# POOL's queue issues the later heads, global values and global queries, and the last seven weight splits stand one per slot

## Chip, cores and metric

One core of one Trainium2 chip runs the whole kernel. The metric is the time of one execution on the device in microseconds, and the number compared is the median of several runs.

## What is computed

The input is attention with a window and a few global tokens, followed by a two-layer feed-forward block. There are 8 batches of 8 heads with 512 local and 32 global tokens and head dimension 64.

```
s_g   = scale * q_g @ concat(k_g, k_l).T
out_g = softmax(s_g) @ concat(v_g, v_l)
s_ll  = where(|i - j| <= 32, scale * q_l @ k_l.T, -1e9)
a_l   = softmax(concat(scale * q_l @ k_g.T, s_ll))
out_l = a_l @ concat(v_g, v_l)
x = concat(out_g, out_l), heads side by side   # 4352 rows of 512
h = max(x @ w_in, 0)                           # w_in 512 x 2048
out = (h * h) @ w_out                          # w_out 2048 x 512
```

Queries, keys and values are float32. The weights are float64; the chip gets each as two 32-bit words and rebuilds a float32 from them.

## The kernel before

**Slots.** The work runs in slots t = 0, 1, 2 ... A slot holds one "head" t, which is half of one head of one batch (256 queries), 128 of them in all, and one eighth m = t - 9 of a block of 256 rows of the feed-forward part (17 blocks, the first of them in slots 9 to 16). Within a slot PE transposes the probabilities of head t-1 (tile `pt`), computes the scores of head t (`s`), two halves of the first matrix product (`h`), the product of probabilities and values of head t-1 (`xa`), the scores of the global queries (`gs`) and the second matrix product of eighth m-1 (`o`). ACT and DVE make what PE needs next: the softmax (`prob`, `st`), copies of `pt` into `ph` and `pl`, the activated rows `r`, `gh`, `gl`, and so on.

**Two halves of each number.** Heads up to 15 and the first block are computed in plain float32. From head 16 and from block 1 on, each operand is split into a rounded half and the rest: for a head, `split_head` makes `hi` and `lo` from `raw` with one ACT copy and three DVE subtractions; for a weight, `w_split` makes the pair `ws` from `wf` with one ACT copy and one DVE subtraction. There are 32 weight chunks. The table PLAN says at which of four places of a slot a chunk is rebuilt ("b") or split ("s"); `w_need` makes up what a product needs before the table has come to it.

**Loads.** `load_head(t)` brings head t into `raw`. Heads from 16 on use a pool of two buffers with the tag "raw", and it is called two slots ahead. The last rebuilt weight, `wf31`, takes one of these two buffers (`w_abs`), and holds it until it is split. `g_load(t)` brings the global queries of the next four heads (`qr`, one buffer) in slots t = 3, 7, 11 ..., and from t = 15 on copies them with ACT and DVE into `qgz`; this stands directly behind `split_head(t+1)`. `g_load_v` brings the global values (`gv`, one buffer). SP's queue issues all of these, the weights and the stores of the results.

**Order.** From slot 17 on (FREE), PE, DVE and ACT take their instructions in the order in which the program writes them, through the class InOrder; before that, and on SP's and POOL's queues throughout, a scheduler orders them. Recorded instructions all have line 52, the helper's.

Of the kernel before, what the change touches and what calls it, by code (L numbers as in the profile page):

```python
# [16 lines left out]
P = 128  # L17
# [9 lines left out]
LAG = 9  # L27
NPLAIN = 16

PLAN = [",,,b", "b,,,b", "b,,,b", "b,,b,", "b,,b,", "b,,b,", "b,,b,", "b,b,,b", "b,b,,b", "bb,bb,bb,bb", "bb,bb,bb,bb", "bbs,bb,bbs,bbs", "bbs,bbs,bbs,bbs", "bbs,bbs,bbs,bbs", "bbs,bbs,bs,s", "ss,s,s,s", "ss,s,s,s", "s,,s,", "s,,s,", "s,,s,", "s,,s,", "s,,s,", "s,,s,"]  # L30
FREE = (17, 17, 17)
LOOK = 2
SQ = (2, 3, 4, 5, 14, 15)
# [4 lines left out]
def f(ap):  # L38
    return ap.bitcast(F32)
# [19 lines left out]
def attention_moe(  # L59
# [8 lines left out]
):  # L68
    nc = tc.nc
    pe, ve, ac = InOrder(tc, nc.tensor), InOrder(tc, nc.vector), InOrder(tc, nc.scalar)  # L70
    PSUM = bass.MemoryType.PSUM
    cp = ctx.enter_context(tc.tile_pool(name="cp", bufs=1))
    wp = ctx.enter_context(tc.tile_pool(name="wp", bufs=WCH))
    p2 = ctx.enter_context(tc.tile_pool(name="p2", bufs=2))
    p1 = ctx.enter_context(tc.tile_pool(name="p1", bufs=1))
    ps_h = ctx.enter_context(tc.tile_pool(name="ps_h", bufs=2, space=PSUM))
    ps_o = ctx.enter_context(tc.tile_pool(name="ps_o", bufs=1, space=PSUM))
    ps_a = ctx.enter_context(tc.tile_pool(name="ps_a", bufs=1, space=PSUM))

    heads = {}  # L80

    def plain(t):
        return t < NPLAIN
# [3 lines left out]
    def w_take(n):  # L87
        w_bufs["free"] -= n

    def load_head(t):  # L90
        if plain(t):
            w_take(1)
            raw = wp.tile([P, 1024], F32, tag="w", name=f"raw{t}")[:, :PK]
        else:
            raw = p2.tile([P, PK], F32, tag="raw", name=f"raw{t}")
        if t == 0:
            nc.sync.dma_start(raw[:, : QC + KC], pk[t, :, : QC + KC])
        else:
            nc.sync.dma_start(raw, pk[t])
        heads[t] = dict(raw=raw)  # L100

    load_head(0)
    con = cp.tile([P, P + 4 * WIN], F32, name="con")

    half = P + 2 * WIN
    nc.sync.dma_start(con[:, P:half], consts[:, P:half])
    load_head(1)
    nc.sync.dma_start(con[:, :P], consts[:, :P])
    nc.sync.dma_start(heads[0]["raw"][:, QC + KC :], pk[0, :, QC + KC :])
    load_head(2)  # L110
    load_head(3)
    ident, masks = con[:, :P], con[:, P:]
# [4 lines left out]
    sg = cp.tile([P, 2, 640], F32, name="sg")  # L117
    qgz = cp.tile([P, 512], F32R, name="qgz")
    prob = [cp.tile([P, 2 * WIN], F32, name=f"prob{i}") for i in range(2)]
    pt = ps_a.tile([P, 512], F32, name="pt")  # L120
    nc.gpsimd.memset(f(qgz), 0.0)
    nc.gpsimd.memset(sg[:, :, 608:], 0.0)
    nc.vector.memset(pt[96:, 256:], 0.0)

    def split_head(t):
# [139 lines left out]
    def g_load(t):  # L265

        b, grp = t // 16, (t // 4) % 2

        def cols(z, j):
            return bass.AP(z.tensor, z.offset + 64 * j, [list(z.ap[0]), [256, 2], [160, 2], [1, 32]])  # L270

        src = qg[b, grp].rearrange("p (a b) n -> p a b n", a=2)
        if plain(t):
            qz = p1.tile([P, 512], F32, tag=("ph", "gvl", "gvh", "ph")[t // 4], name=f"qz{t}")
            nc.gpsimd.memset(qz, 0.0)
            qr = p1.tile([P, 2, 2, 32], F32, tag="qr", name=f"qr{t}")
            (nc.sync if t else nc.scalar).dma_start(qr, src)
            nc.gpsimd.tensor_copy(cols(qz, 0), qr)
        else:
            qz = qgz  # L280
            qr = p1.tile([P, 2, 2, 32], F32, tag="qr", name=f"qr{t}")
            nc.sync.dma_start(qr, src)
            ac.copy(cols(qgz, 0), qr)
            ve.tensor_sub(cols(qgz, 1), qr, f(cols(qgz, 0)))
        state["qz"] = qz
# [26 lines left out]
    def g_load_v(t, pair):  # L312
        gv = p1.tile([P, 640], F32, tag="gv", name=f"gv{t}_{pair}").rearrange("p (c n) -> p c n", c=5)
        src = vg[t // 16, 2 * ((t // 4) % 2) + pair]
        nc.sync.dma_start(gv, src.rearrange("(c p) n -> p c n", p=P))
        state["gv"] = gv

    def g_split_v(t, pair):
# [238 lines left out]
    def w_tick(t, place):  # L557
        if t < len(PLAN):
            for c in PLAN[t].split(",")[place]:
                {"b": w_pass, "s": w_chunk}[c]()  # L560
# [14 lines left out]
    def w_done(m):  # L575
        w_used.update(range(4 * m, 4 * m + 4))
        for i in (4 * m, 4 * m + 2):
            w_free(i)

    g_load(0)  # L580
    for t in range(4, 8):
        load_head(t)
# [6 lines left out]
    for t in range(NSTEP + LAG + 1):  # L589
# [55 lines left out]
        if live:  # L645
            if t % 2 == 1:
                g_evac(t)
            if t % 4 == 3 and t + 1 < NT:
                g_load(t + 1)
        elif t == NT:  # L650
            state["gs"] = None
        if live and t % 4 == 3 and (t // 8) % 2 == 1:
            d = t if t % 8 == 3 else t + 2
            for at, *job in (
                (d, 2, g_load_v, 0),
                (d + 1, 3, g_soft),
                (d + 1, 1, g_exp),
                (d + 2, 3, g_norm),
                (d + 2, 1, g_tr),
                (d + 3, 5, g_tr_last),  # L660
                (d + 3, 4, g_rest),
                (d + 3, 3, g_split_v, 0),
                (d + 3, 2, g_load_v, 1),
                (d + 3, 1, g_av, 0),
                (max(d + 4, 17), 3, g_x, 0),
                (d + 5, 2, g_split_v, 1),
                (max(d + 6, 17), 1, g_av, 1),
                (max(d + 7, 18), 3, g_x, 1),
            ):
                place, job, *args = job  # L670
                jobs.setdefault((at, place), []).append((job, t, *args))
# [21 lines left out]
        if 8 * NGR - 2 <= m < 8 * NGR:  # L693
            cols = (slice(0, 224), slice(224, HALF))[m % 2]
# [76 lines left out]
```

## Time and profile before

| | |
|---|---|
| median of 3 runs | 1068.83 us (1068.21 to 1069.07) |
| the profiled execution's own time | 1068.82 us |
| its span, first to last instruction | 1067.0 us |
| PE busy | 1050.4 us |
| DVE busy | 856.3 us |
| ACT busy | 753.1 us |
| POOL busy | 3.9 us in 14 instructions |

The profile gives, for one execution, when each instruction of each engine ran, and for an engine's idle time what ended it. An issue of a transfer is an instruction of a queue (SPq); its landing is told apart from it. Slots can be read from PE's row of instructions: each begins with the four transposes into `pt`.

### The profile page before, as it was taken

To read this page: it belongs to the slowest core of one execution; us is meant where nothing else is said; L and a number is where in the kernel's file an instruction comes from. 1 tells how busy PE (TensorE), PEld (TensorE's weight loads), DVE (VectorE), ACT (ScalarE), POOL (GpSimd) and SP (SyncE) were. 2 spreads that over 40 slices of the span, in tenths; PEclk is the share of its full clock that TensorE was granted. 3 is DMA by queue.
4 is the path that set the end of the run, shared out by engine and by line. 5 is a ranking of instruction groups with operands and counts; after the bars stand their busy time and mean duration, and the time that the engine had idled before them with its cause. 6 is when DMAs were issued, how large, how long until landed. Compare 5 with 4: busy or idle time off the path is not lost.

```text
span 1067.0 us, 21142 instructions
## 1 busy us (share of the span) xinstructions
PE 1050.4 (98%) x7568; PEld 941.7 (88%) x7568; DVE 856.3 (80%) x2687; ACT 753.1 (71%) x1901; POOL 3.9 (0%) x14
## 2 busy tenths in 40 slices
PE   7999999999999999999999999999999999999998
PEld 6776889999998989998999989999999989999896
DVE  5698988898888989988888888888888888874321
ACT  5898877778777776778777777777777787774322
POOL 1000000000000000000000000000000000000000
PEclk9999999999999999999999999999999999999999
DMA  9772132223222322222322222223221322201000
GB/s 372 310 263 74 57 106 76 71 80 98 68 89 64 103 65 83 74 91 77 94 71 82 86 72 76 90 66 100 78 89 55 94 86 66 88 29 33 13 20 20
DMA packets 54312, 96.78 MB, mean 91 GB/s; under 512 B 4288, under 2 KB 29376, under 8 KB 54208
## 3 DMA queue, kind: packets, MB, share of 16 engines
q1 hardware_dynamic: 54064, 95.37, 27.2%
q8 instruction: 60, 0.98, 0.4%
q14 instruction: 44, 0.36, 0.1%
q10 hardware_dynamic: 144, 0.07, 0.0%
HBM read 86.51 MB, written 8.91 MB: 89 GB/s over the span
## 4 chain that ended last, share of the span: by engine, by line
PE 87%; ACT 7%; DVE 4%; issue 1%; DMA 0%; ACTq 0%
PE o L52 33%; PE h L52 32%; PE xa L52 7%; PE s L52 6%; PE pt L52 5%; PE gxo L52 2%; PE gs L52 2%; ACT prob L52 1%; DVE prob L52 1%; ACT r L52 1%; ACT ph L52 1%; ACT hi L52 1%; ACT ot L52 1%; PE gt L52 1%; ACT sg L52 0%
## 5 line engine op out<-in xcount | busy, mean ns | idle before, releaser
L52 PE MATMUL h<-x_h,ws 128*128 128x256 f32 x2048 | 388.9, 283 | 0.0
L52 PEld LDWEIGHTS h<-x_h,ws 128*128 128x128 f32 x2048 | 327.0, 191 | 0.5
L52 PE MATMUL o<-ws,gh 128*128 128x512 f32 x1024 | 321.3, 395 | 0.0
L52 PE MATMUL h<-x_l,ws 128*128 128x256 f32 x1024 | 289.1, 282 | 0.1
L52 PEld LDWEIGHTS o<-ws,gh 128*128 128x128 f32 x1024 | 185.5, 188 | 34.6
L52 PE MATMUL o<-ws,gl 128*128 128x512 f32 x512 | 202.6, 396 | 0.0
L52 PEld LDWEIGHTS h<-x_l,ws 128*128 128x128 f32 x1024 | 195.9, 191 | 0.9 <-DVE x_l L52 0.4
L52 ACT CAST ph<-pt 128x256 fp32r<-128x256 f32 x448 | 141.1, 341 | 67.7 <-PE pt L52 60.8
L52 ACT ACTIVATE prob<-prob,st 128x224 f32<-128x224 f32 x270 | 127.8, 475 | 61.2 <-DVE st L52 59.1
L52 ACT ACTIVATE r<-h 128x512 f32<-128x512 f32 x136 | 81.4, 599 | 112.3 <-PE h L52 112.3
L52 PEld LDWEIGHTS o<-ws,gl 128*128 128x128 f32 x512 | 96.2, 188 | 22.7
L52 DVE CUSTOM_DVE_ANT_0 prob<-s,con 128x224 f32<-128x224 f32 x256 | 90.0, 386 | 24.5 <-PE s L52 23.2
L52 DVE TENSOR_TENSOR gl<-r,gh 128x512 fp32r<-128x512 f32 x128 | 87.9, 686 | 23.3 <-ACT gh L52 20.5
L52 ACT CAST hi<-raw 128x864 fp32r<-128x864 f32 x112 | 102.5, 915 | 1.4
L52 DVE TENSOR_TENSOR r<-h,r 128x512 f32<-128x512 f32 x82 | 56.7, 692 | 51.9 <-ACT r L52 50.6
L52 PE MATMUL xa<-ph,hi 128*64 128x128 f32 x448 | 87.3, 238 | 1.6 <-DVE ph L52 1.2
L52 DVE TENSOR_TENSOR hi<-raw,hi 64x352 fp32r<-64x352 f32 x224 | 82.5, 368 | 6.4
L52 ACT CAST gh<-r 128x512 fp32r<-128x512 f32 x128 | 79.1, 618 | 9.1 <-DVE r L52 8.7
L52 DVE TENSOR_TENSOR ph<-pt,ph 64x128 fp32r<-64x128 f32 x224 | 79.6, 355 | 7.0
L52 DVE TENSOR_TENSOR lo<-raw,hi 128x448 fp32r<-128x448 f32 x112 | 69.6, 622 | 15.3 <-ACT hi L52 12.5
L52 PE MATMUL pt<-con,prob 128*128 128x128 f32 (+1 forms) x512 | 78.2, 274 | 0.7 <-ACT prob L52 0.5
L52 DVE TENSOR_SCALAR prob<-prob,st 128x224 f32<-128x224 f32 x242 | 70.7, 334 | 4.1
(80 smaller groups left out, 1572.7 us busy)
## 6 DMA issues: line engine op xcount, KB each, us to landing
raw<-in_pk_dram SPq DMA_DIRECT2D x127, 432.0 KB, 3.2
wr<-in_w_dram SPq DMA_DIRECT2D x32, 512.0 KB, 7.9
gv<-in_vg_dram SPq DMA_DIRECT2D x32, 320.0 KB, 3.3
out_dram<-ot SPq DMA_DIRECT2D x32, 256.0 KB, 2.2
qr<-in_qg_dram SPq DMA_DIRECT2D x31, 64.0 KB, 2.8
out_dram<-ot SPq DMA_DIRECT2D x8, 64.0 KB, 1.7
con<-in_consts_dram SPq DMA_DIRECT2D x2, 224.0 KB, 5.1
raw<-in_pk_dram SPq DMA_DIRECT2D x1, 304.0 KB, 3.2
```

Of the source, the lines that this page charges most:

```text
L52: r = method(*args, **kwargs)
```

## The change

Three things are edited. POOL's instructions go through InOrder as well, so that its queue runs in the order in which the program is written. The loads of heads from 16 on, of all global values and of the global queries from slot 15 on are issued by POOL's queue instead of SP's. In PLAN, the weight splits from slot 17 on stand differently: before, two in each of slots 17, 18 and 19 and one in slot 20 were left to make; now one stands in each of slots 17, 19, 20, 21 and 22 and two in slot 23.

```diff
-... "ss,s,s,s", "s,,s,", "s,,s,", "s,,s,", "s,,s,", "s,,s,", "s,,s,"]
+... "ss,s,s,s", "s,,,", ",,,", "s,,,", "s,,,", "s,,,", "s,,,", "s,,s,"]
...
+    po = InOrder(tc, nc.gpsimd)
...
-            nc.sync.dma_start(raw, pk[t])
+            (nc.sync if plain(t) else po).dma_start(raw, pk[t])
...
-    nc.gpsimd.memset(f(qgz), 0.0)
-    nc.gpsimd.memset(sg[:, :, 608:], 0.0)
+    po.memset(f(qgz), 0.0)
+    po.memset(sg[:, :, 608:], 0.0)
...
         if plain(t):
...
-            nc.gpsimd.memset(qz, 0.0)
+            po.memset(qz, 0.0)
...
-            nc.gpsimd.tensor_copy(cols(qz, 0), qr)
+            po.tensor_copy(cols(qz, 0), qr)
         else:
...
-            nc.sync.dma_start(qr, src)
+            po.dma_start(qr, src)
             ac.copy(cols(qgz, 0), qr)
             ve.tensor_sub(cols(qgz, 1), qr, f(cols(qgz, 0)))
...
     def g_load_v(t, pair):
...
-        nc.sync.dma_start(gv, src.rearrange("(c p) n -> p c n", p=P))
+        po.dma_start(gv, src.rearrange("(c p) n -> p c n", p=P))
```

What follows are rows of the two programs as they are queued, with the semaphores that a row waits for; a number after a tile's name is the head or slot that it belongs to, the one after the underscore only counts tiles. DMAHW and DMASW are semaphores of landings.

The first place is the queue that loads. On SP's queue before, the global queries of heads 20 to 23 (`qr20`) stood among the weights:

```order
L406 DMA wr18_546<-in_w_dram 128x1024 [waits DMAHW6_49,PE_49]
L406 DMA wr19_568<-in_w_dram 128x1024 [waits DMAHW7_49,PE_49]
L282 DMA qr20_1358<-in_qg_dram 128x128 [waits DMAHW2_49,DMAHW0_49,DVE_49]
L406 DMA wr20_598<-in_w_dram 128x1024 [waits DMAHW1_49]
L406 DMA wr21_616<-in_w_dram 128x1024 [waits PE_49]
```

That is long before head 20 itself, which follows here, with the queries `qr24` ahead of head 22:

```order
L99 DMA raw20_1155<-in_pk_dram 128x864 [waits DMAHW0_49,DMAHW3_49,DVE_49,Activation_49]
L99 DMA raw21_1271<-in_pk_dram 128x864 [waits DMAHW3_49,DMAHW4_49,DVE_49,Activation_49]
L282 DMA qr24_1790<-in_qg_dram 128x128 [waits DVE_49]
L315 DMA gv15_1_1479<-in_vg_dram 128x5x128 [waits DMAHW7_49,DVE_49,Activation_49]
L99 DMA raw22_1388<-in_pk_dram 128x864 [waits DVE_49,PE_49]
L99 DMA raw23_1513<-in_pk_dram 128x864 [waits DMAHW4_49,DVE_49,Activation_49]
L99 DMA raw24_1612<-in_pk_dram 128x864 [waits DMAHW1_49,DMAHW7_49,DVE_49,Activation_49]
```

On POOL's queue now, at the same place of the program:

```order
L52 DMA raw20_1152<-in_pk_dram 128x864 [waits DMASW6_49,DVE_49,Activation_49]
L52 DMA raw21_1262<-in_pk_dram 128x864 [waits DMASW0_49,DVE_49,Activation_49]
L52 DMA qr20_1349<-in_qg_dram 128x128 [waits DMASW4_49]
L52 DMA raw22_1376<-in_pk_dram 128x864 [waits DMASW1_49,DVE_49,Activation_49]
L52 DMA gv15_1_1467<-in_vg_dram 128x5x128 [waits DMASW7_49]
L52 DMA raw23_1501<-in_pk_dram 128x864 [waits DMASW3_49,DVE_49,Activation_49]
L52 DMA raw24_1603<-in_pk_dram 128x864 [waits DMASW5_49,DVE_49,Activation_49]
L52 DMA raw25_1705<-in_pk_dram 128x864 [waits DMASW6_49,DVE_49,Activation_49]
L52 DMA qr24_1787<-in_qg_dram 128x128 [waits DMASW2_49]
L52 DMA raw26_1826<-in_pk_dram 128x864 [waits DVE_49,PE_49]
```

The queries `qr20` moved behind head 21 and `qr24` behind head 25. Each head from 18 to 25 now waits for the last reads (DVE, ACT) of the head directly in front of it, since they share one buffer; before, that ended with head 21, and head 22 took the buffer of `wf31`, which now goes to head 26 (the row that waits for DVE and PE).

The second place is ACT's queue in slot 19, from the evacuation of `xa18` to the copy of `pt` for head 19. Before:

```order
L52 CAST x_h_88<-xa18_1330 64x256 [waits PE_49]
L52 CAST hi20_1350<-raw20_1155 128x864 [waits DMAHW3_49]
L52 COPY sg_91<-gs18_1232 64x288 [waits PE_49]
L52 CAST qgz_92<-qr20_1358 128x2x2x32
L52 CAST gh10_1374<-r10_1345 128x512 [waits Activation_49]
L52 CAST ws30_1378<-wf30_835 128x512 [waits DVE_49]
L52 CAST pth15_1386<-gt15_1381 128x512 [waits PE_49]
L52 CAST ph19_1413<-pt_95 128x256 [waits PE_49]
```

Now:

```order
L52 CAST x_h_88<-xa18_1321 64x256 [waits PE_49]
L52 CAST hi20_1341<-raw20_1152 128x864 [waits DMASW0_49]
L52 COPY sg_91<-gs18_1226 64x288 [waits PE_49]
L52 CAST qgz_92<-qr20_1349 128x2x2x32 [waits DMASW2_49]
L52 CAST gh10_1365<-r10_1336 128x512 [waits Activation_49]
L52 CAST pth15_1374<-gt15_1369 128x512 [waits PE_49]
L52 CAST ph19_1401<-pt_95 128x256 [waits DVE_49,PE_49]
```

The split `ws30` left this place, and the copy into `qgz` got a wait for the landing of `qr20`.

The third place is ACT's queue in slot 23, from the same evacuation on. Before:

```order
L52 CAST hi24_1782<-raw24_1612 128x864 [waits DMAHW1_49]
L52 COPY sg_91<-gs22_1673 64x288 [waits PE_49]
L52 CAST qgz_92<-qr24_1790 128x2x2x32 [waits DMAHW5_49]
L52 CAST gh14_1806<-r14_1777 128x512 [waits DVE_49]
L52 ACTIVATE gxs15_1_1824<-gxo15_1_1810,gst15_1198 64x128 [waits PE_49]
L52 CAST ph23_1850<-pt_95 128x256 [waits PE_49,Activation_49]
```

Now:

```order
L52 CAST hi24_1779<-raw24_1603 128x864 [waits DMASW6_49]
L52 COPY sg_91<-gs22_1667 64x288 [waits PE_49]
L52 CAST qgz_92<-qr24_1787 128x2x2x32 [waits DMASW0_49]
L52 CAST gh14_1803<-r14_1774 128x512 [waits DVE_49]
L52 CAST ws31_1807<-wf31_864 128x512 [waits Activation_49]
L52 ACTIVATE gxs15_1_1824<-gxo15_1_1810,gst15_1195 64x128 [waits PE_49]
L52 CAST ph23_1850<-pt_95 128x256 [waits PE_49]
```

The order is the same but for the split `ws31`, which came in from slot 20.

More of the change, by code (lines that the diff above doesn't have):

```diff
@@ L28 @@
 NPLAIN = 16
-PLAN = [",,,b", "b,,,b", "b,,,b", "b,,b,", "b,,b,", "b,,b,", "b,,b,", "b,b,,b", "b,b,,b", "bb,bb,bb,bb", "bb,bb,bb,bb", "bbs,bb,bbs,bbs", "bbs,bbs,bbs,bbs", "bbs,bbs,bbs,bbs", "bbs,bbs,bs,s", "ss,s,s,s", "ss,s,s,s", "s,,s,", "s,,s,", "s,,s,", "s,,s,", "s,,s,", "s,,s,"]
+PLAN = [",,,b", "b,,,b", "b,,,b", "b,,b,", "b,,b,", "b,,b,", "b,,b,", "b,b,,b", "b,b,,b", "bb,bb,bb,bb", "bb,bb,bb,bb", "bbs,bb,bbs,bbs", "bbs,bbs,bbs,bbs", "bbs,bbs,bbs,bbs", "bbs,bbs,bs,s", "ss,s,s,s", "ss,s,s,s", "s,,,", ",,,", "s,,,", "s,,,", "s,,,", "s,,,", "s,,s,"]
 FREE = (17, 17, 17)
```

## Prediction

> **What bounds the kernel now.** I read the page's span and busy times first.
>
> ```profile
> span 1067.0 us, 21142 instructions
> PE 1050.4 (98%) x7568; PEld 941.7 (88%) x7568; DVE 856.3 (80%) x2687; ACT 753.1 (71%) x1901; POOL 3.9 (0%) x14
> ```
>
> PE idles for 16.6 us in all, so nothing that only feeds it faster can gain more. Next I cut the run into slots, at PE's four transposes, and asked for each engine's busy time in stretches: slots 16, 19 and 20, then slots 35 and 36, which hold the same jobs as 19 and 20 but no weight splits. The columns are the stretch in us, its length, and the busy time of PE, PEld, DVE, ACT and POOL.
>
> ```profile
> 97.51:106.97 9.46, 9.01 (x41) 6.31 (x40) 7.52 (x20) 7.64 (x18) 0.00 (x0) 1.00 0.27 81
> ...
> 122.95:131.57 8.62, 7.96 (x60) 7.15 (x59) 8.11 (x26) 7.80 (x20) 0.00 (x0) 1.00 0.18 53
> 131.57:141.36 9.79, 9.08 (x71) 7.66 (x69) 8.74 (x26) 7.73 (x19) 0.00 (x0) 1.00 0.35 105
> ...
> 156.09:164.13 8.04, 8.04 (x68) 7.45 (x67) 7.61 (x24) 5.24 (x14) 0.00 (x0) 1.00 0.33 98
> ...
> 246.93:255.05 8.12, 7.96 (x60) 7.14 (x59) 6.60 (x25) 6.46 (x17) 0.00 (x0) 1.00 0.17 54
> 255.05:263.65 8.60, 8.55 (x70) 7.55 (x69) 7.35 (x23) 6.59 (x16) 0.00 (x0) 1.00 0.32 98
> ```
>
> Slots 19 and 20 take 8.62 + 9.79 = 18.41 us, their counterparts 8.12 + 8.60 = 16.72 us. In slot 19 DVE is busy for 8.11 us, about as long as a slot without splits lasts: there, for a moment, DVE and ACT set the pace. The excess, 1.69 us, is what weight splits cost after slot 16.
>
> Then the loads: the page's issues with the median from issue to landing, what SP's queue waited for, the landings of `qr` (minimum, median, maximum), and POOL's two kinds of instruction, which have nothing to do with loads but are all that POOL does now.
>
> ```profile
> raw<-in_pk_dram SPq DMA_DIRECT2D x127, 432.0 KB, 3.2
> ...
> qr<-in_qg_dram SPq DMA_DIRECT2D x31, 64.0 KB, 2.8
> ```
>
> ```profile
> SPq L99 <- DVE hi L52: 626.7, 109, 21.1
> ...
> DMA to landing us min/median/max: 2.5/2.8/9.2
> ...
> 0.73 0.52 POOL L121 MEMSET qgz<- 128x512 f32 x1 [0.29 <-POOLq L761]
> ...
> 3.81 0.29 POOL L278 COPY qz<-qr 128x128 f32<-128x128 f32 x1 [1.08 <-DMA qr<-in_qg_dram]
> ```
>
> SP's queue stood still in 109 head loads until DVE had read the old head; a load there holds whatever is queued behind it, and I take POOL's queue to do the same.
>
> **The change part by part.** *The splits.* Three of them leave slots 17 to 19, one stays in slot 20, and slots 21, 22 and 23 get one, one and two. Out come up to 1.69 us; since slot 20 keeps its one, I take 1.3. Slot 23 (156.09 above) has DVE busy for 7.61 of 8.04 us, and two splits of about 0.6 us each (rows below) don't fit into that; but one falls behind the wait below and is counted there, so I put 0.3 us on slots 21 to 23.
>
> *The wait for `qr20`.* Before, these queries were on the chip long ahead. Now their load stands behind that of `raw21`, which waits until DVE has read `raw20`. ACT copies `qr20` into `qgz` before that moment:
>
> ```profile
> 130.85 0.30 ACT L52 CAST qgz<-qr 128x128 fp32r<-128x128 f32 x1
> 131.57 0.61 ACT L52 CAST ws<-wf 128x512 fp32r<-128x512 f32 x1
> ...
> 131.08 0.75 DVE L52 TENSOR_TENSOR hi<-raw,hi 64x352 fp32r<-64x352 f32 x2
> 133.15 0.69 DVE L52 TENSOR_TENSOR ws<-wf,ws 128x512 fp32r<-128x512 f32 x1
> ```
>
> DVE's last read ends at 131.08 + 0.75 = 131.83 and ACT wants the queries at 130.85, 0.98 us earlier. Call P the time from that read to their landing. Then ACT stands still for P + 0.98 us, with `gh`, `pth` and `ph` queued behind it, and DVE with its own part of `qgz`, then `gl`, `pth`, `pl` and `ph`.
>
> P is two issues and a landing, and no row shows POOL issue one. From below: the shortest landing, 2.5, and two issues of 0.3 (POOL's copy) make 3.1. From above: the landing of the head ahead of it, 3.2, and then a whole landing of 2.5, as if the two ran one after the other, make 5.7; the 9.2 belongs to the first slots, when all weights are loaded too. Less than nothing is excluded, since the order forces a landing after the read. I choose 4.2: two issues of 0.5, as POOL's 0.52 memset, and the 3.2 of the head's load, with which the queries share the engines. The Trainium skill, "DMA: Bandwidth & Descriptors", section on latency and other measured facts, gives about 1 us to the first byte for a transfer issued by GpSimd against about 0.6 by SP: by that P is 4.6 and, with both waits, the sum 0.8 us longer; no run here shows it yet.
>
> What that costs PE is read from slots 35 and 36, where no split is in the way:
>
> ```profile
> 254.12 0.30 ACT L52 CAST qgz<-qr 128x128 fp32r<-128x128 f32 x1
> ...
> 255.73 1.30 ACT L52 CAST ph<-pt 128x256 fp32r<-128x256 f32 x4
> 257.05 0.26 ACT L52 CAST pth<-gs 64x128 fp32r<-64x128 f32 x1
> ...
> 254.35 0.75 DVE L52 TENSOR_TENSOR hi<-raw,hi 64x352 fp32r<-64x352 f32 x2
> ...
> 257.34 0.29 DVE L52 TENSOR_TENSOR pth<-gs,pth 64x128 fp32r<-64x128 f32 x1 [0.24 <-ACT pth L52]
> ...
> 258.92 0.74 DVE L52 TENSOR_TENSOR ph<-pt,ph 64x128 fp32r<-64x128 f32 x2
> ...
> 259.81 0.31 PE L52 MATMUL xa<-ph,hi 128*64 128x256 f32 x1
> ```
>
> From the copy to the end of DVE's last piece of `ph`, at 259.66, there are 5.54 us, and PE uses it 0.15 us later: PE has no lead here. Some 0.55 us of the 5.54 are short idle times ahead of ACT's and DVE's `pth` that a late start takes up (0.24 of them in the row above, the rest ahead of ACT's). So PE is late by P + 0.98 - 0.55, rounded P + 0.4 = **4.6 us**.
>
> *The wait for `qr24`.* The same in slot 23, since `raw25` waits for `raw24`: both are in one buffer as long as `wf31`, now split in slot 23, holds the other.
>
> ```profile
> 162.26 0.30 ACT L52 CAST qgz<-qr 128x128 fp32r<-128x128 f32 x1
> 162.46 0.62 ACT L52 CAST gh<-r 128x512 fp32r<-128x512 f32 x1
> 164.34 0.36 ACT L52 ACTIVATE gxs<-gxo,gst 64x128 f32<-64x128 f32 x1 [1.26 <-PE gxo L52]
> 164.85 1.29 ACT L52 CAST ph<-pt 128x256 fp32r<-128x256 f32 x4 [0.15 <-PE pt L52]
> ...
> 162.51 0.77 DVE L52 TENSOR_TENSOR hi<-raw,hi 64x352 fp32r<-64x352 f32 x2
> ...
> 164.00 0.68 DVE L52 TENSOR_TENSOR gl<-r,gh 128x512 fp32r<-128x512 f32 x1
> ...
> 166.63 0.74 DVE L52 TENSOR_TENSOR ph<-pt,ph 64x128 fp32r<-64x128 f32 x2
> ...
> 168.40 0.28 PE L52 MATMUL xa<-ph,hi 128*64 128x256 f32 x1
> ```
>
> DVE's read ends at 163.28; with P = 4.2 the copy starts at 167.48 instead of 162.26, 5.2 us late. Behind it come `gh` to 168.3, the split `ws31` with its 0.5 us of ACT to 168.8, `gxs` and then `ph` from 169.2 to 170.5; DVE, with `gl` and 0.6 us of `ws31`, ends its last piece of `ph` at about 171.7. PE wanted it at 168.40: **3.35 us** late, or P - 0.85. Here PE has a lead of some 2 us, since ACT and DVE idle for 1.26 and more after the copy.
>
> *Later groups.* From head 26 on there are two buffers again, and the queries' load waits for a head one slot older:
>
> ```profile
> 185.42 0.77 DVE L52 TENSOR_TENSOR hi<-raw,hi 64x352 fp32r<-64x352 f32 x2
> ...
> 192.20 0.30 ACT L52 CAST qgz<-qr 128x128 fp32r<-128x128 f32 x1
> ```
>
> That read ends at 186.19, 6.0 us ahead of the copy: more than P, so nothing is paid. If the cover went, the price would be P - 6.0, less PE's lead of 2, in each of 25 groups. *The heads with one buffer*, 22 to 25, have to land in less time than before:
>
> ```profile
> 148.51 0.77 DVE L52 TENSOR_TENSOR hi<-raw,hi 64x352 fp32r<-64x352 f32 x2
> ...
> 153.84 0.92 ACT L52 CAST hi<-raw 128x864 fp32r<-128x864 f32 x1
> ```
>
> From 149.28 to 153.84 there are 4.56 us for a landing of 3.2 and an issue of 0.5. That holds, with 0.9 to spare. *Global values* are loaded three slots ahead of use and cost nothing; the same for the stores, alone on SP's queue with the weights now.
>
> *Before slot 17* the scheduler put ACT's and DVE's instructions in another order, as the weights no longer share a queue with heads. PE's order there is the same but for one swap. In slot 16 PE idles for 9.46 - 9.01 = 0.45 us; I take 0, and 1.5 us to either side, about three such gaps.
>
> The sum: -1.3 + 0.3 + 4.6 + 3.35 = 6.95, rounded 7.0 us on the profiled execution's own 1068.82 (span 1067.0 and 1.8 around it). That equals the median of 1068.83, so the forecast is **1075.8 us**. With P = 3.1 the waits are 3.5 and 2.25, the sum 4.75 and the time 1073.6; with P = 5.7 they are 6.1 and 4.85, the sum 9.95 and the time 1078.8.
>
> **The rivals.** *A: faster, because ACT gets to the copy later than I think.* If the scheduler's new order before slot 17 and the three splits less let PE run ahead of ACT and DVE, the copy is reached after the landing and both waits are hidden. This decides once ACT's copy comes P = 4.2 us behind DVE's read; today it comes 0.98 us ahead of it, and the very next row of DVE waits for the same copy. Then only the 1.3 us and slot 16's 0.45 remain: 1067.1 us. Against it: copy and read hang on the same `hi` copy of ACT, so they move together.
>
> *B: POOL's queue is slow, and the wait comes back in every group.* If issuing waits for gaps in DVE's work, P grows by a DVE row of up to 0.7 us per issue, to 5.6, which is in the range above. At P = 7 the sum is 12.75 and the time 1081.6; beyond P = 8 all 25 later groups pay, and with P = 9 they add 25 x 1.0 us to 16.55 us, for 1110 us. The Trainium skill, "SBUF — State Buffer", section "Who interferes with whom", states such a rule: a transfer issued by GpSimd is starved while DVE runs in a mode that takes both pairs of ports, and one issued by SP is not. Against it here: in the two places DVE itself comes to stand still behind the copy, and the rows ahead are subtractions of two operands.
>
> *C: only one wait shows.* If PE's lead in slot 24 is 4 us rather than 2, the second wait is hidden, and with P near 3.1 the sum is -1.3 + 0.3 + 3.5 = 2.5: 1071.3 us; less still, if the early slots gain.
>
> **How the numbers follow.** A measurement of this kernel can tell 0.2%, some 2.1 us, from no change. My forecast's mechanism has a chance of 0.70, A 0.08, B 0.13 (half of it within 1081.6), C 0.09. A is faster in 0.07 of its 0.08 and otherwise the same; of C, 0.06 is the same and 0.03 slower; forecast and B are slower. So faster 0.07, same 0.07, slower 0.86. The range goes from 1071.3, where C begins, to 1081.6, the middle of B; the forecast's own is 1072.1 (1073.6 less the early 1.5) to 1080.3.
>
> **What would show it.** In the changed profile ACT's copy into `qgz` in slots 19 and 23 would have an idle time of 4 to 6 us ahead of it, ended by the landing of `qr`; PE would idle for some 3 to 5 us ahead of `xa` in slots 20 and 24; slots 17 to 19 would be without PE's 0.66 us; from slot 26 on every slot would have its old length. I am wrong if these waits aren't there, if the idle time ahead of `qgz` is there but PE runs on, or if ACT waits for `qr` or `raw` in later groups too.

## The result, and the profile after

The changed kernel takes 1079.63 us (median of five runs, 1079.39 to 1080.52) against 1068.83 us (1068.21 to 1069.38) before: 10.8 us more, a ratio of 1.0102 with a 95% interval of 1.0088 to 1.0116. The profiled execution took 1080.52 us, 11.7 more than that of before.

Both waits are there. The page of the changed kernel, its span and busy times:

```profile
span 1078.8 us, 21127 instructions
...
PE 1055.1 (98%) x7568; PEld 945.4 (88%) x7568; DVE 857.2 (79%) x2687; ACT 752.3 (70%) x1901; POOL 106.9 (10%) x186
```

PE is busy 4.7 us longer than before, with as many products; 7 of the 11.7 us are idle time, and the rest is the same work done more slowly. Where ACT and DVE waited for the queries (time in all, how often, the longest):

```profile
ACT qgz L52 <- DMA qr<-in_qg_dram: 11.3, 2, 6.0
...
DVE qgz L52 <- ACT qgz L52: 8.1, 2, 4.1
```

Twice, and not once in a later group. The rows of DVE, POOL, ACT and PE around both places, from the timeline of the changed kernel (start, duration, operation, and in brackets the idle time ahead):

```profile
130.34 0.75 DVE L52 TENSOR_TENSOR hi<-raw,hi 64x352 fp32r<-64x352 f32 x2
...
131.64 0.54 POOL L52 DMA_DIRECT2D raw<-in_pk_dram  x1 [6.74 <-DVE sg L52]
132.17 0.54 POOL L52 DMA_DIRECT2D qr<-in_qg_dram  x1
...
135.38 0.30 ACT L52 CAST qgz<-qr 128x128 fp32r<-128x128 f32 x1 [5.29 <-DMA qr<-in_qg_dram]
...
137.68 0.25 PE L52 MATMUL xa<-ph,hi 128*64 128x128 f32 x1 [2.40 <-DVE ptl L52]
...
139.91 0.37 PE L52 MATMUL xa<-pl,hi 128*64 128x128 f32 x1 [1.93 <-DVE pl L52]
...
169.49 0.77 DVE L52 TENSOR_TENSOR hi<-raw,hi 64x352 fp32r<-64x352 f32 x2
...
174.35 0.30 ACT L52 CAST qgz<-qr 128x128 fp32r<-128x128 f32 x1 [5.98 <-DMA qr<-in_qg_dram]
...
176.38 0.37 PE L52 MATMUL xa<-ph,hi 128*64 128x128 f32 x1 [2.62 <-ACT ph L52]
...
177.76 0.37 PE L52 MATMUL xa<-pl,hi 128*64 128x128 f32 x1 [0.91 <-DVE pl L52]
```

DVE's last read of `raw20` ends at 131.09, and ACT has the queries at 135.38: the time called P is 4.3 us here, and 4.1 us (170.26 to 174.35) at the second place, against the 4.2 that the prediction chose. The sum is the forecast one, its parts are not: POOL starts the head's issue 0.55 us after the read, which no term held, and takes 0.54 us over it, and 3.2 us after the start of their own issue the queries have landed. The profile counts a landing from the start of its issue, so the prediction's second issue of 0.5 us was already in its 3.2; that the lag of 0.55 us stands in its place is luck.

Slots 19, 20 and 23 to 25 by the stretches view (the columns are those of the prediction; the three numbers behind POOL's are the granted clock, the share of the time in which the transfer engines were busy, and GB/s):

```profile
122.95:131.05 8.10, 7.95 (x60) 7.14 (x58) 7.19 (x26) 6.14 (x16) 0.55 (x1) 1.00 0.21 57
131.05:146.56 15.51, 11.18 (x71) 9.48 (x69) 9.27 (x26) 7.91 (x19) 1.33 (x3) 0.78 0.10 33
...
161.19:169.81 8.62, 8.39 (x68) 7.44 (x67) 7.75 (x23) 4.87 (x13) 0.54 (x1) 1.00 0.16 53
169.81:183.49 13.68, 10.14 (x57) 8.65 (x56) 8.99 (x28) 6.38 (x16) 1.60 (x3) 0.75 0.23 69
183.49:190.78 7.29, 7.29 (x56) 6.69 (x55) 5.62 (x19) 4.97 (x14) 0.54 (x1) 1.00 0.20 63
```

Slot 20 grew from 9.79 to 15.51 us and slot 24 from 7.30 to 13.68; every slot from 26 on has its old length to within some hundredths. But slot 20 idles for 4.3 us only, and PE's 71 matmuls, which kept it busy for 9.08 us before, now take 11.18. The clock column says why. Cut finer:

```profile
135.50:138.22 2.72, 0.30 (x2) 0.19 (x2) 1.59 (x3) 2.64 (x8) 0.00 (x0) 1.00 0.00 0
138.22:141.63 3.41, 1.72 (x9) 1.57 (x10) 2.58 (x10) 2.12 (x7) 0.00 (x0) 0.50 0.00 0
141.63:145.05 3.42, 3.42 (x9) 2.65 (x8) 3.23 (x10) 3.03 (x6) 0.00 (x0) 0.50 0.00 0
145.05:146.56 1.51, 1.51 (x18) 1.29 (x16) 1.36 (x3) 0.00 (x0) 0.26 (x1) 1.00 0.00 0
...
175.76:179.17 3.41, 1.88 (x11) 1.57 (x12) 3.24 (x14) 3.15 (x11) 0.54 (x1) 0.50 0.28 57
179.17:182.59 3.42, 3.42 (x10) 2.65 (x10) 3.19 (x9) 1.84 (x3) 0.00 (x0) 0.50 0.17 73
```

After each wait the granted clock is 0.50 for 6.83 us, and PE works at half speed there. The prediction has no term for this.

### The profile page after: what moved, and what is told of

It reads as the page before. It is cut to its first block, busy times and chain, and to the rows that moved or that the text cites. A ratio compares the mean times of both kernels' runs of the same rounds, so it can differ in the third digit from the quotient of the medians.

```text
span 1078.8 us, 21127 instructions
## 1 busy us (share of the span) xinstructions
PE 1055.1 (98%) x7568; PEld 945.4 (88%) x7568; DVE 857.2 (79%) x2687; ACT 752.3 (70%) x1901; POOL 106.9 (10%) x186
## 4 chain that ended last, share of the span: by engine, by line
PE 83%; ACT 9%; DVE 6%; issue 1%; DMA 1%; POOL 0%; ACTq 0%; DVEq 0%
PE o L52 32%; PE h L52 31%; PE xa L52 6%; PE s L52 5%; PE pt L52 4%; PE gxo L52 2%; PE gs L52 2%; DVE prob L52 2%; ACT prob L52 2%; ACT r L52 1%; ACT ph L52 1%; ACT hi L52 1%; ACT wf L52 1%; ACT ot L52 1%; ACT pth L52 1%
## 5 line engine op out<-in xcount | busy, mean ns | idle before, releaser
L52 POOL DMA_DIRECT2D raw<-in_pk_dram x112 | 60.8, 542 | 718.2 <-DVE hi L52 315.6
```

Of the source, the lines that this page charges most:

```text
L52: r = method(*args, **kwargs)
```

## The experiments

**Are the two waits the cause, and is it the order of the queue or POOL itself?** Four kernels take one part each.

The first leaves everything as changed but the queue of the global queries:

```diff
-            po.dma_start(qr, src)
+            nc.sync.dma_start(qr, src)
```

> The changed kernel with one thing undone: the global queries of heads from 16 on are issued by SP's queue again, heads and values stay on POOL's. My theory: the whole loss comes from the two landings of queries that stand behind heads 21 and 25 on POOL's queue (4.3 and 3.5 us of PE's idle time) and from the halved clock that follows each (some 2.6 us each); then both go, and the time falls from 1079.6 to about 1067.7 us, a little under the 1068.8 of before. Rival 1, POOL's transfers cost by themselves (a longer issue and landing for every head): it stays above 1075. Rival 2, the late splits and the heads with one buffer cost: it stays above 1075 too.

It took 1070.56 us (1069.79 to 1072.72), against 1068.61 before in the same series: a ratio of 1.0023, 1.0014 to 1.0032.

The second leaves the queries on POOL's queue, but issues them ahead of the head's load and not behind it (a function `g_query(t + 1)`, called just ahead of `load_head(t + 2)`):

```diff
+        if t % 4 == 3 and NPLAIN <= t + 1 < NT:
+            g_query(t + 1)
         if NPLAIN <= t + 2 < NT:
             load_head(t + 2)
```

> The changed kernel with the load of the queries written ahead of the head's load in the same slot, so that on POOL's queue it stands in front of the head that waits, and all else as changed, on POOL's queue. My theory: no wait for queries, the clock stays, about 1067.7 us. Rival 1 (POOL's transfers cost by themselves): above 1075. If only the place on the queue matters and not the queue, this and the run with the queries on SP's queue are equal within 0.5 us.

1069.99 us (1069.33 to 1070.48), ratio 1.0013, 1.0004 to 1.0022. Slots 20 and 24 take 9.17 and 7.60 us here, at a clock of 1.00. So POOL's queue may issue the queries; it is their place behind a waiting load that costs over 9 of the 10.8 us.

The third has the changed queues with the old table of splits:

```diff
-PLAN = [..., "s,,,", ",,,", "s,,,", "s,,,", "s,,,", "s,,,", "s,,s,"]
+PLAN = [..., "s,,s,", "s,,s,", "s,,s,", "s,,s,", "s,,s,", "s,,s,"]
```

> The changed kernel with the table of splits as before, so the last weight leaves its buffer in slot 20 and only head 21 still waits for the head directly in front of it. My theory: the wait for the queries of head 20 stays, that for head 24's goes, and the clock falls once: 1068.8 + 4.3 + 2.6, about 1075.7 us, where the idle time alone would give 1073.1. Rival 1 (POOL's transfers cost by themselves): about the 1079.6 of the changed kernel. Rival 2 (the late splits cost): 1068.8.

1074.93 us (1074.67 to 1075.27), ratio 1.006, 1.0047 to 1.0072. One wait is left, since `wf31` gives its buffer back in slot 20 here and the heads around slot 23 have two again. The waits view of this kernel:

```profile
ACT qgz L52 <- DMA qr<-in_qg_dram: 5.3, 1, 5.3
```

One wait costs 6.3 us; idle time alone would have made about 4.3 (slot 20 idles for 5.04 us here and for 0.71 before).

The fourth has the old queues with the new table of splits:

> The kernel before with only the new table of splits; all loads stay on SP's queue, where the queries stand early. My theory: the 1.7 us of slots 19 and 20 come back for the most part and slot 23 costs some 0.6: about 1067.7 us. Rival 2 (late splits and heads with one buffer up to head 25 cost): above 1070.

1069.17 us (1068.84 to 1069.42), ratio 1.0005, 0.9997 to 1.0014: the gain of over a microsecond that the prediction gave to the thinned splits is not there. Slots 19, 20, 23, 24 and 25 of this kernel:

```profile
122.93:131.04 8.11, 7.96 (x60) 7.15 (x59) 7.20 (x26) 6.97 (x18) 0.00 (x0) 1.00 0.20 57
131.04:140.22 9.18, 8.77 (x71) 7.54 (x69) 7.93 (x24) 7.10 (x17) 0.00 (x0) 1.00 0.33 91
154.95:163.58 8.63, 8.40 (x68) 7.44 (x67) 7.74 (x23) 6.26 (x16) 0.00 (x0) 1.00 0.30 92
163.58:171.19 7.61, 7.50 (x57) 6.79 (x56) 7.15 (x25) 5.12 (x13) 0.00 (x0) 1.00 0.38 125
171.19:179.31 8.12, 7.52 (x55) 6.71 (x54) 7.11 (x22) 5.02 (x15) 0.00 (x0) 1.00 0.20 57
```

Slots 19 and 20 gain 0.51 and 0.61 us, as hoped for (8.62 and 9.79 before). But slots 23, 24 and 25, at 8.05, 7.30 and 7.30 us before, lose 0.58, 0.31 and 0.82: the splits cost there what they had cost earlier, and a little more. This kernel, which differs from the changed one in the queues alone, is the base for the waits below. It also explains why the first two kernels came out above the 1067.7 expected: their slots 13 to 16, where the scheduler orders ACT, DVE and the loads anew, take 1.6 and 0.9 us longer than before's 38.70 us; with the 0.6 us of the splits that makes 1070.8 and 1070.1. What in the new order costs this wasn't tested. In the changed kernel itself the same four slots take 38.51 us.

**Is the slow clock a consequence of PE's idle time, and what is it worth?** The first try fills the waits with products that nobody reads, ahead of the group that waits:

```diff
+FILL = {19: 9, 23: 7}
...
+        for _ in range(FILL.get(t, 0)):
+            pe.matmul(xa, con[:, :64], con[:, 128:384], start=True, stop=True, skip_group_check=True)
```

> The changed kernel, with 9 matmuls of float32 that nobody reads put ahead of PE's xa group of slot 20 and 7 ahead of that of slot 24; they fall into the two waits and keep PE busy there, and each row of ACT, DVE and the queues stands as it was. They are computed in addition and overwritten, so the output is unchanged. Theory (each wait costs its idle time and, behind it, 2.4 to 2.6 us of halved clock): the granted clock stays at 1.00 in slots 20 and 24, PE's four o groups take 0.7 us again instead of 1.3, and the time falls by about 5 us, from 1079.6 to 1074.6. Rival (the slow products behind the waits have another cause, such as late operands): no change, 1079.6.

1080.75 us (1079.4 to 1082.19), ratio 1.0115, 1.0101 to 1.0129: no gain, and at first sight the rival's case. PE's row of these products, and the clock in the 2 us from their start, show another reason:

```profile
137.10 5.73 PE L53 MATMUL xa<-con 128*64 128x256 f32 x18 [2.35 <-DVE ptl L53]
```

```profile
137.00:139.00 2.00, 1.90 (x5) 1.12 (x6) 1.17 (x8) 0.76 (x3) 0.00 (x0) 0.51 0.00 0
```

(L53 is the same helper, one line further down.) The products waited 2.35 us themselves, until ACT and DVE, standing behind the queries, let them go; by then the clock was at half. They ran at that speed until 140.44, took 5.73 us in all, and held up the work that they were to keep warm. So the experiment did not fill the wait. Nor was it the same in each execution: two of the four show a mean clock of 0.996 and took 1082.1 and 1082.2 us, the profiled one among them, and two show 0.999, as kernels without a halved stretch do, and took 1079.4. Half as many did a little better, because they ended about when the waited-for data came:

> The same with 4 and 3 such matmuls, so that PE stands idle for about half as long as in the changed kernel, some 2.5 us in slot 20 and 2.2 us in slot 24. If the clock falls only after an idle time longer than that, the time is that of the full fill, 1074.6; if each us idle takes its share of clock, 1077; if any wait of this length halves it, 1079.6.

1078.43 us (1078.3 to 1078.93), ratio 1.0094, 1.0080 to 1.0108; none of the three values expected, since 2.3 us of idle time were left at the same place and halved the clock again, for one stretch of 3.4 us per wait and not two. One of the four executions shows a clock of 0.999, and at 1078.50 us it is no faster than the others.

The second try puts the products ahead of `h`, where PE still had all that it needed:

```diff
+FILL = {20: 9, 24: 8}
...
+        for _ in range(FILL.get(m + LAG, 0) if j == 0 else 0):
+            pe.matmul(hp[:, 0, :], con[:, :128], con[:, 128:384], start=True, stop=True)
```

> The changed kernel with 9 and 8 matmuls of float32 that nobody reads, this time ahead of the first h group of slots 20 and 24, where PE still has everything it needs; they go into h's own accumulator and are overwritten. The first try put them ahead of xa, where they themselves waited 2.35 us for ACT (which stood behind the queries), so that the clock had halved before they began, and PE ran them at half speed. At about 0.43 us each they take 3.9 and 3.4 us of PE's 4.3 and 3.5 us of idle time. Theory (the clock falls when PE was idle for most of one of the fixed stretches of 3.41 us in which it seems to be set anew): no stretch at half clock, slot 20 takes about 13 us instead of 15.5, slot 24 about 11 instead of 13.7, and the time is 1074.5 to 1075.5. Rival (the halving is not PE's idleness but the wait as such, or the late operands): 1079.6. If filling delays r and with it DVE, it is longer still.

Slots 20, 24 and 25 of this kernel:

```profile
131.03:145.23 14.20, 12.99 (x88) 11.10 (x87) 8.04 (x24) 7.92 (x19) 1.06 (x2) 1.00 0.11 36
168.57:180.59 12.02, 11.31 (x74) 9.98 (x73) 7.31 (x25) 6.34 (x16) 1.60 (x3) 1.00 0.26 79
180.59:188.72 8.13, 7.52 (x55) 6.71 (x54) 7.12 (x22) 5.03 (x15) 0.54 (x1) 1.00 0.19 56
```

The clock stays at 1.00, so its fall is PE's idle time and nothing else about the waits. But the kernel takes 1078.76 us (1078.44 to 1079.01), ratio 1.0092, 1.0075 to 1.0109, and not the 1074.5 to 1075.5 expected. Slot 20 falls by 1.3 us and not 2.5, slot 24 by 1.7, and slot 25 rises by 0.85 to the 8.12 us that it has in the kernel with the new table alone. While PE is slow, DVE and ACT catch up; at full clock PE waits for them instead, at `gxo` of slot 20 for 0.36 us and at the scores of slot 25 for 0.61. The slow clock is worth 1.31 + 1.66 - 0.85 = 2.1 us in the profiled executions, less than the 5 us by which it keeps PE busier (2.41 and 2.64 us in slots 20 and 24, against the kernel with the new table alone).

This kernel, without the clock's part, measures the waits by themselves, against the one with the new table alone: slot 20 is 14.20 - 9.18 = 5.0 us longer, slot 24 12.02 - 7.61 = 4.4 us. The unread products don't add to that: the last product of `xa` starts 9.79 and 8.94 us into slots 20 and 24 here, and 9.73 and 8.82 us in the changed kernel.

**How much idle time does it take?** In the kernel before, the copy into `qgz` is made several times over, so that ACT is late by a chosen time at six places with the same work; no queue is touched:

```diff
+REP = {36: 8, 52: 11, 68: 14, 84: 17, 100: 20, 116: 23}
...
-            ac.copy(cols(qgz, 0), qr)
+            for _ in range(1 + REP.get(t, 0)):
+                ac.copy(cols(qgz, 0), qr)
```

> The kernel before, in which ACT makes the copy of the global queries into qgz not once but 9, 12, 15, 18, 21 and 24 times, in slots 35, 51, 67, 83, 99 and 115, which hold the same work; nothing else is changed, no queue is touched. At about 0.27 us a copy ACT is 2.2, 3.0, 3.8, 4.6, 5.4 and 6.2 us late, and PE, by the prediction's reading of slots 35 and 36 (0.55 us of slack), idles for about 1.6, 2.4, 3.2, 4.0, 4.8 and 5.6 us more in the slot behind. Theory: up to some length, between 1.6 and 4.0 us, a slot grows by its idle time alone, and beyond it by 2.4 to 2.8 us more, at whatever length. Rival: the further loss grows evenly with the idle time, from about 1.0 to 3.5 us. Second rival: only the loads on POOL's queue slow PE down, and every slot grows by its idle time alone. Altogether 21.6 us of idle time: with four losses of 2.6 us about 1100, without any 1090.

The one timed run took 1107.04 us. The first, the third and the last of the delayed slots (8.60 us in the kernel before, 0.05 of it idle):

```profile
255.35:267.85 12.50, 10.43 (x71) 8.97 (x69) 8.67 (x25) 8.92 (x24) 0.00 (x0) 0.86 0.23 69
...
508.11:523.15 15.04, 11.34 (x71) 9.61 (x69) 8.66 (x25) 10.70 (x30) 0.00 (x0) 0.77 0.23 62
...
896.58:913.53 16.95, 10.43 (x71) 8.92 (x69) 8.44 (x25) 13.38 (x39) 0.00 (x0) 0.80 0.18 51
```

They idle for 2.07, 3.70 and 6.52 us, and beyond that take 1.9, 2.8 and 1.9 us longer: a loss comes in each, and it does not grow with the idle time. The rival that it grows evenly falls, and so does the one that only POOL's loads bring it about. Where the clock falls and rises is seen in rows across the edges, for the first three delays:

```profile
262.00:262.50 0.50, 0.34 (x5) 0.23 (x3) 0.33 (x1) 0.50 (x3) 0.00 (x0) 0.93 0.00 0
...
265.50:266.00 0.50, 0.50 (x3) 0.42 (x2) 0.50 (x1) 0.42 (x1) 0.00 (x0) 0.66 1.08 302
388.30:388.80 0.50, 0.14 (x2) 0.15 (x3) 0.47 (x2) 0.49 (x3) 0.00 (x0) 0.93 0.00 0
...
392.00:392.50 0.50, 0.50 (x3) 0.36 (x3) 0.44 (x3) 0.50 (x2) 0.00 (x0) 0.86 0.26 77
514.60:515.10 0.50, 0.00 (x0) 0.00 (x0) 0.35 (x2) 0.11 (x1) 0.00 (x0) 0.92 0.00 0
...
521.60:522.10 0.50, 0.50 (x3) 0.45 (x2) 0.48 (x1) 0.00 (x0) 0.00 (x0) 0.75 0.00 0
```

A mean of 0.93 over 0.5 us means half speed in its last 0.07 us, so the falls are at 262.43, 388.73 and 515.02, the rises at 265.84, 392.14 and 521.85. The slow stretches last 3.41, 3.41 and 6.83 us, and the falls lie 126.30 and 126.29 us apart, 37 times 3.413 each. The two falls of the changed kernel, at 138.22 and 175.76, are 37.54 us apart, 11 times 3.413. So the clock is set anew at fixed instants, 3.41 us apart, and not a certain time after PE fell idle.

Shorter delays of the same kind:

```diff
-REP = {36: 8, 52: 11, 68: 14, 84: 17, 100: 20, 116: 23}
+REP = {36: 3, 52: 4, 68: 5, 84: 6, 100: 7, 116: 6}
```

> The kernel before with the copy of the global queries made 4, 5, 6, 7, 8 and again 7 times in slots 35, 51, 67, 83, 99 and 115. From the longer delays (idle time 2.0 us at 9 copies, 0.32 us more for each further one) PE's idle time is expected at about 0.4, 0.7, 1.1, 1.4, 1.7 and 1.4 us. Theory of fixed stretches of 3.41 us with a bound on their idle share: the longer delays halved the clock with 1.9 us idle in a stretch, and kept it halved with 1.3, so idle times up to about 1 us should cost only themselves, and those above can go either way, by how a stretch cuts them; where the clock falls, the slot grows by a further 1.7 us, and the starts of half clock lie whole multiples of 3.41 us apart. Rival (any idle time of half a us or more costs clock): every slot grows by 1 to 2 us more than it idles.

None of the six lost clock (1077.30 us, one run). The longest single idle time of the short delays is 1.58 us (ending at 755.04), the shortest that cost clock among the longer ones 1.91 us (ending at 261.61). But in the kernel with the queries on SP one of 2.07 us, from 77.46 to 79.53, left the clock at 1.00. So the length of a single wait does not decide.

How it lies to the fixed instants does. Where these lie can be read in every trace, since the clock also falls at the end, when PE has nothing left to do. In the changed kernel that last fall comes at 1076.88, 275 stretches of 3.4133 us after the first. In the kernel with the queries on SP it comes at 1065.66, and 290 and 289 such stretches earlier, at 75.80 and 79.21, two of the instants lie; the second cuts the 2.07 us into 1.75 and 0.32. Here are the stretch between the two and the next one, and then two stretches of the kernel of the following question, which has the changed queues and one split moved (its first fall, at 139.00, is ten stretches ahead of 173.14):

```profile
75.80:79.21 3.41, 1.66 (x4) 0.38 (x2) 3.32 (x7) 3.41 (x9) 0.00 (x0) 1.00 0.79 290
79.21:82.62 3.41, 3.09 (x19) 2.86 (x20) 3.41 (x11) 2.99 (x8) 0.00 (x0) 1.00 0.72 249
...
173.14:176.55 3.41, 1.62 (x13) 1.27 (x11) 1.86 (x6) 2.37 (x7) 0.00 (x0) 1.00 0.06 24
176.55:179.96 3.41, 2.41 (x11) 2.10 (x12) 3.14 (x16) 3.15 (x9) 0.54 (x1) 0.50 0.45 130
```

With 1.75 us of idle time in its stretch the clock stayed, with 1.79 it was halved. Cut at these instants, from the first 10 us on, the 14 traces of this case have no stretch at full clock with 1.75 us or less before a fall, and none with 1.79 us or more without one. The 1.58 us of the short delays are cut in two (0.91 and 0.66), the 1.91 us lie in one stretch. A halved stretch was followed by another where PE idled in it for 1.00 us or more (9 of 24), and by full clock where it idled for 0.22 us or less (15). So in these traces the bound is about half of a stretch, summed over its idle times.

The Trainium skill, "TensorE: Matmul & The Clock Gate", Part 1: The HAM clock gate, describes a window of 3413 ns that runs on freely and after which the clock is halved or doubled. The distances above agree to the hundredth of a us. It calls for an idle window of about 3.4 us ahead of a fall, and there this case's rows differ: 1.79 us of idle time within a window sufficed.

**Why did the second wait cost more than forecast?** The first of the two splits of slot 23 is moved to slot 18:

```diff
-PLAN = [..., "s,,,", ",,,", "s,,,", "s,,,", "s,,,", "s,,,", "s,,s,"]
+PLAN = [..., "s,,,", "s,,,", "s,,,", "s,,,", "s,,,", "s,,,", ",,s,"]
```

> The changed kernel with the first of the two splits of slot 23 put into slot 18, which held none; queues as changed. Theory: the wait for qr24 cost more than forecast (4.4 us without the clock against 3.35) because this split pushes DVE's last read of raw24, and with it the loads of raw25 and qr24, from 0.85 us ahead of the start of slot 24 to 0.45 us behind it. Then the read comes ahead of the start again, slot 23 takes 8.05 us again instead of 8.62, slot 24 about 1.2 us less than 13.68, and the time falls by 1.5 to 2 us to about 1078. Rival (the second wait was longer for another reason, such as ws31 behind it): slot 24 stays at about 13.7 and only slot 23's 0.6 us go, 1079.0.

1078.87 us (1078.72 to 1080.58), ratio 1.0093, 1.0078 to 1.0109; too near to the changed kernel's 1.0102 to tell the times apart. The rows tell more. DVE's last read of `raw24`, and slots 23 and 24:

```profile
169.10 0.77 DVE L52 TENSOR_TENSOR hi<-raw,hi 64x352 fp32r<-64x352 f32 x2
```

```profile
161.92:170.48 8.56, 8.34 (x69) 7.53 (x67) 7.99 (x24) 4.46 (x12) 0.60 (x2) 1.00 0.17 54
170.48:183.73 13.25, 10.46 (x57) 8.90 (x56) 8.38 (x25) 6.38 (x16) 1.93 (x4) 0.74 0.24 72
```

The read ends 0.61 us ahead of the start of slot 24; in the changed kernel it ends 0.45 us behind it (170.26 against 169.81). So the split does push the read, by 1.06 us, and the first `o` comes 8.42 us into the slot instead of 9.31. The rest of the expectation failed: slot 23 stays at 8.56 us, slot 18's split costs slot 19 0.5 us, and the halved stretch, which lay otherwise here, took back half of what slot 24 had gained.

**Can the splits gain anything by themselves?** Two more tables in the kernel before, with its own queues. One has two splits in each of slots 17 and 18, one in 19, none in 20, one in 21 and 22; the other moves the single split of slot 20 to slot 21:

```diff
-PLAN = [..., "s,,s,", "s,,s,", "s,,s,", "s,,s,", "s,,s,", "s,,s,"]
+PLAN = [..., "s,,s,", "s,,s,", "s,,,", ",,,", "s,,,", "s,,,"]
+PLAN = [..., "s,,s,", "s,,s,", "s,,s,", ",,,", "s,,,"]
```

> The kernel before, with the queues as they were and only the seven last splits placed anew: two in each of slots 17 and 18 as before, one in slot 19, none in slot 20, one in each of slots 21 and 22. Theory (a split costs only where ACT and DVE have no time left: in slot 20, the second one in slot 19, the second one in slot 23 and its followers; it is free in 17, 18, 21 and 22): slot 19 falls from 8.62 to 8.10, slot 20 from 9.79 to 8.60, and the time by 1.7 us to 1067.1, below both kernels. Rival (the thinning gains nothing wherever it is put, since PE's next wait takes it up): 1068.8 or more.

> The kernel before, queues and all, with one edit: the single weight split of slot 20 stands in slot 21. The runs so far: with no split in slot 20 it took 8.62 us in place of 9.79, and a single split in slot 21 or 22 added nothing to that slot itself, though slots 22 and 23 grew by 0.8 us when slot 22 held one too. Theory: slot 20 falls by 1.2 us, the others stay, and the time by that to 1067.5, 0.1% below both kernels, which is at the edge of what can be told. Rival (any split costs its 0.6 us of DVE wherever it goes): 1068.2 to 1068.8.

They took 1068.14 us (1067.36 to 1068.54; ratio 0.9995, 0.9986 to 1.0004) and 1068.29 us (1067.87 to 1069.01; ratio 0.9996, 0.9987 to 1.0005): no difference that can be told. Slots 20 and 23 of the first, and slots 20, 22 and 23 of the second:

```profile
131.04:139.67 8.63, 8.44 (x71) 7.54 (x69) 7.58 (x24) 6.67 (x17) 0.00 (x0) 1.00 0.30 88
...
154.60:163.20 8.60, 8.36 (x69) 7.54 (x67) 8.11 (x25) 5.18 (x14) 0.00 (x0) 1.00 0.31 93
```

```profile
131.49:140.70 9.21, 8.86 (x70) 7.69 (x69) 8.16 (x25) 7.20 (x18) 0.00 (x0) 1.00 0.30 85
...
148.07:155.67 7.60, 7.50 (x55) 6.71 (x54) 6.87 (x21) 5.60 (x14) 0.00 (x0) 1.00 0.19 60
155.67:163.72 8.05, 8.05 (x68) 7.46 (x67) 7.62 (x24) 5.25 (x14) 0.00 (x0) 1.00 0.34 98
```

Slot 20 falls from 9.79 to 8.63 and 9.21 us, and a split in slot 21 makes slot 22 0.27 us longer, one in slot 22 makes slot 23 0.55 us longer. A split that seems free in its own slot is paid for, in part at least, in the next one.

## Why the prediction was right or wrong

The direction, both waits, their places and their single occurrence came as forecast, and 1079.63 lies in the range; 1075.8 was 3.8 us low. By the steps, on the profiled executions (slots 19 to 25 take 55.78 us before and 67.83 after):

| step | forecast, us | measured, us | from |
|---|---|---|---|
| splits | -1.3 + 0.3 = -1.0 | +0.6 | new table alone against before, slots 19 to 25 |
| wait for `qr20` | 4.6 | 5.0 | slot 20, early fill against new table alone |
| wait for `qr24` | 3.35 | 4.4 | slot 24, the same |
| halved clock | no term | 2.1 | slots 20, 24, 25, changed kernel against early fill |
| sum | 6.95 | 12.1 | 67.83 - 55.78 = 12.05 |

- *The missing term* is the step that failed most in the profiled execution: an idle PE was priced at its idle time. Behind both waits it worked at half clock for 6.83 us. That costs 2.1 us net in the profiled execution. In the median it is less: the five executions have a mean clock of 0.993 twice (1080.2 and 1080.5 us) and 0.996 three times (1079.4 to 1079.6 us), and between the medians of the changed kernel and of the early fill lie only 0.9 us. By the medians the splits and the two waits make up 9.9 of the 10.8 us (early fill against before), and the largest error of a single term is that of the splits.
- *The splits.* "Out come up to 1.69 us; since slot 20 keeps its one, I take 1.3" priced the slots that they left; "0.3 us on slots 21 to 23" looked for their new cost in the slots that they went to, and not in the one behind. There 1.1 us of it lie, in slots 24 and 25.
- *The wait for `qr20`.* P was right (4.3), but by luck in its parts: an issue counted twice stood for a lag that had no term. Of the 0.55 us of slack that the late start should have taken up, only some 0.3 were there: the copy came 5.26 us later against PE's slot than in slot 35 and 36, and `xa` was late by 5.0.
- *The wait for `qr24`.* P was right again (4.1). What failed is the place of DVE's read, 0.85 us ahead of slot 24 in the kernel before, which the prediction kept; the split newly placed ahead of it moves it by 1.06 us.
- *Later groups, heads with one buffer, global values, stores:* nothing, as forecast. No slot from 26 on is longer by more than 0.02 us.
- *Before slot 17:* forecast 0 with 1.5 us to either side. The changed kernel is 0.02 us ahead at slot 17. That this was luck as much as insight shows in the first two experiments, where the same scheduler lost 1.6 and 0.9 us.
- *The rivals.* A fell, as ACT's copy and DVE's read moved together. B fell on its mechanism: P is 4.1 to 4.3, no later group waits, and 1079.63 comes from the clock and the splits, though it is near B's first figure. (That figure is itself 0.2 us too high: with P = 7 the waits are 7.4 and 6.15, the sum 12.55 and the time 1081.4.) C fell, as both waits show. The rule of the Trainium skill, "SBUF — State Buffer", section "Who interferes with whom", isn't put to the test by these P: DVE stood still while POOL issued both loads (131.64 to 132.71, with DVE idle from 131.57 to 135.71). Over the whole run little of it can be there: with DVE busy for 79% of the span the heads landed in 3.5 us from POOL against 3.2 from SP. The Trainium skill, "DMA: Bandwidth & Descriptors" (latency and other measured facts), lets the first bytes of GpSimd's transfers come 0.4 us later than SP's. The trace agrees as far as landings tell: they come 0.3 us (heads) and 0.4 us (queries) later from POOL in the median. P stayed below the 4.6 worked out from it because the queries' 3.2 and 3.0 us at the two places are still no more than SP's head load took.

## What to carry to other kernels

An in-order queue makes a transfer wait for whatever the one ahead of it waits for; a small, early-needed load goes ahead of the big load that waits for a buffer, and then it does not matter which engine issues it. Price an idle time of PE that can take up half of a stretch of 3.41 us (some 1.75 us here) not at its length alone: look at the granted clock behind it, and let the price end where another engine takes over as the last. Work moved out of a tight slot is to be priced in the slot behind its new place, against the order of the reads there.

## What the runs showed of the hardware that was not expected

- The granted clock is set at instants 3.413 us apart. 1.79 us of idle time between two of them halved it, 1.75 us did not, and 2.07 us in one piece did not where an instant cut them into 1.75 and 0.32. It stayed halved for 3.41 or 6.83 us, and the work inside took nearly twice as long: three products of `o` 1.28 us instead of 0.70.
- Unread products placed where they wait themselves held the clock in two of four executions only; in the profiled one they began at half speed and took 5.73 us for 18 passes, which take 4.06 us at full clock. Placed where PE still had its operands, they held it in all four.
- POOL's queue issues the load of a head 0.55 us after the read that frees its buffer and takes 0.54 us over it; in the trace of before SP's queue did so 0.07 us after (`raw21`'s at 131.90, the read's end at 131.83) and took 0.34 us. From issue to landing the heads took 3.2 us in the median from SP and the queries 2.8; the issues of the changed kernel's page:

```profile
raw<-in_pk_dram POOLq DMA_DIRECT2D x112, 432.0 KB, 3.5
...
qr<-in_qg_dram POOLq DMA_DIRECT2D x28, 64.0 KB, 3.2
```

With the loads in the right order this lag of some 0.7 us was covered.
